# Queueing the last pass's matmuls on TensorE in the order of the source, with the block products begun later and at another pace

## The chip, the cores and the metric

One core of a Trainium2 chip runs the whole kernel. The metric is the time of one execution on the device, in microseconds (us); a kernel is timed in several runs, and the median counts. A profiled execution is one more run, whose trace gives every instruction of the engines: TensorE (PE, with its weight loads as PEld), VectorE (DVE), ScalarE (ACT), GpSimd (POOL) and SyncE (SP), which issues the DMAs.

## What is computed

Three layers follow one another, all in 32-bit floats. The change touches only the last.

1. Retention over 4 x 8 heads of 576 tokens: scores, times a decay that depends on the distance, times v. It gives x, 2304 tokens by 512.
2. A gated layer: `silu(x @ w_gate) * (x @ w_val) @ w_out`, 1536 hidden columns.
3. A squared-ReLU layer on its result:

```python
h = x @ w_in                # 2304 x 512 @ 512 x 2048
r = np.maximum(h, 0.0)
g = r * r
return (g @ w_out)          # 2304 x 2048 @ 2048 x 512
```

## The kernel before, in words

**Arithmetic.** Every 32-bit operand is split into a high part and a low part (`split`: ACT casts the high part, DVE subtracts it for the low part), and a product of two operands is three matmuls: high x high, high x low, low x high. Large products are made by a Strassen-Winograd scheme: seven products of half-size blocks instead of eight, with sums of operands before and sums of results after.

**Passes.** The last layer works through the 2304 tokens in three passes of 768. A pass has eight *systems* (`systems`, one for each 256 hidden columns). The last pass holds the systems 40 to 47, and `turn_over` is 40. A system is seven **slots**, `slot(n, i)` (line 660), i being the number of the Strassen product: six matmuls of 384 columns each, then the evictions. Products 1, 6, 7, 4 build up in a bank called g, 5 and 3 in a bank v, 2 in a bank z; a later product of a bank adds to what is there, so it waits until ACT or DVE has read the bank. Slot 4 and slot 3 complete the two halves of the system's hidden block, tiles caa and cab in the trace (the squared ReLU is a DVE operation).

**The second matrix product of the last pass.** For the other passes it is done by `out2`, in tiles of twelve 512-column matmuls, one or two systems later. For the last pass the systems 40 to 45 are taken in pairs, (40, 41), (42, 43), (44, 45), again by the scheme of seven: a pair is named by its odd system, which this text calls block 41, 43 or 45. Each block has three tiles j of 128 tokens, each with seven **block products**, `out3(n, j, at)` (line 885), of six matmuls of 256 columns: 63 products in all. `PRODUCTS` and `at` give their order. A product's hidden operand is ready when POOL has made four sums of the block's tile (`sums2`, line 865, twelve operations for three tiles), and ACT and DVE have split the tile and the sums (`prepare`, line 874, hs_h and hs_l in the trace). The first product of a tile needs no sum, the second does. There are two buffers for the split tiles, so a tile's splits wait for the last product of the tile two places earlier. The weight operands (wt in the trace) are loaded by DMA (`operands2`, line 826); block 43's go into buffers that block 41's last tile leaves, as its products are done. Each product adds to the bank of the product two places earlier, so it waits until that one's result is evicted (ACT or DVE, xy<-oacc). Systems 46 and 47 are not paired by the scheme: `whole` splits them, and `out4` makes and stores the final output in six pieces, of twelve matmuls of 512 columns (the last piece in halves, twice twelve of 256).

**Order of the work.** The loop of the last pass (line 1103) goes over n = 40 to 48 and writes seven slots in each iteration, partly of system n and partly of n - 1 (three in the last), 59 in all. Iterations 40 and 41 also write nine `out2` tiles of the pass before. After the slot (3, 41), the sixth of iteration 42, the sums and splits of block 41 are written. After each slot, `flow` writes as many block products as a formula allows, which counts slots from `begin_at`:

```python
begin_at = 7 * 3 + START
past = slots["n"] - begin_at
flow(min(int(1.5 * past + 0.7 * max(0, past - 28)), 21 * PAIRED // 2))
```

What is left goes after the loop (`flow(len(stream))`, line 1152).

The written order is not each engine's queue. The framework plans every engine's order itself, on an estimated timeline: where an instruction is not ready in the estimate, a later one that is ready goes first. In the text this is the *planner*. The class `Chained` (line 109) wraps the engines; while `chain["on"]` is set, each instruction is tied behind the one before it on its engine (`issue_after`), so that the written order holds. It is set in the first layer only. `self.last` is the instruction that following ones are tied behind, `self.recent` the latest.

Of the kernel before, what the change touches and what calls it, by code (L numbers as in the profile page):

```python
# [56 lines left out]
PRODUCTS = (1, 5, 6, 3, 7, 2, 4)  # L57
SUMS = (6, 5, 4, 7)
PAIRED = 6
START = 4  # L60


TINY = float(np.uint32(0x38000000).view(np.float32))
# [4 lines left out]
def retention_moe_kernel(  # L68
# [13 lines left out]
    def pool(stack, name, bufs, **kw):  # L82
        return stack.enter_context(
            tc.tile_pool(name=name, bufs=bufs, reuse_waits="tile", **kw)
        )
# [21 lines left out]
    chain = {"on": False}  # L107

    class Chained:


        def __init__(self, engine):
            self.engine, self.last, self.recent = engine, None, None

        def __getattr__(self, name):
            op = getattr(self.engine, name)

            def traced(*args, **kw):
                with ExitStack() as behind:
                    if self.last is not None:  # L120
                        behind.enter_context(tc.issue_after(self.last))
                    i = op(*args, **kw)  # L122
                self.recent = i.ins
                if chain["on"]:
                    self.last = i.ins
                return i

            return traced

    pe, dve, act, pool_e, sp = map(Chained, (nc.tensor, nc.vector, nc.scalar, nc.gpsimd, nc.sync))  # L130
# [219 lines left out]
    def build(n):  # L350

        ph, p, k, what = systems[n]
        if p:
            for x in (0, 3, 2, 1):
                w = operand_tile(n, x)
                sp.dma_start(out=w.bitcast(F32), in_=win[ph, k, what, x])
                yield
                if x != 2:
                    yield
            return  # L360
        w0, w1_ = inputs.pop(n)
        if ph == 1:
            for x in (w0, w1_):
                ensure(x, ready)
            w0, w1_ = ready.pop(w0), ready.pop(w1_)

        def to(x, src):
            if x == 4:
                if ph == 1:
                    built[n, "p"] = w = wb_p.tile([P, 2, 256], F32R, tag="p", name="wb")  # L370
                    split(w[:, 0], w[:, 1], src)
                return
            w = operand_tile(n, x)
            split(w[:, 0], w[:, 1], src)
            later.append((win[ph, k, what, x], w.bitcast(F32)))

        s1 = s1_p.tile([P, 256], F32, tag="s1", name="s1")
        for _ in stationary(w0, w1_, s1, to):
            yield
            while later and n:  # L380
                sp.dma_start(out=later[0][0], in_=later.pop(0)[1])
        if ph == 1:
            loads["held"] -= 2
# [352 lines left out]
    def load_out(n, fs):  # L736
        ph, p = systems[n][:2]
        for f in fs:
            key = (ph, "o", f)
            w = wos[f] = wo_p.tile([P, 2, 512], F32R, tag="wo", name="wo")  # L740
            if p:
                sp.dma_start(out=w.bitcast(F32), in_=wsp[key])
                continue
            if ph == 1:
                ensure(key, ready)
                src = ready.pop(key)
                loads["held"] -= 1
                act.copy(w[:, 0], src)
                pool_e.tensor_tensor(out=w[:, 1], in0=src, in1=f32(w[:, 0]), op=ALU.subtract)
            else:  # L750
                ensure(key, stored)
                sp.dma_start(out=w[:, 1].bitcast(F32), in_=wst[key])
                act.copy(w[:, 0], f32(w[:, 1]))
                tt(out=w[:, 1], in0=f32(w[:, 1]), in1=f32(w[:, 0]), op=ALU.subtract)
            sp.dma_start(out=wsp[key], in_=w.bitcast(F32))
# [70 lines left out]
    def operands2(n):  # L826

        k, x, homes = systems[n][2], n - turn_over, []
        for at, i in enumerate(PRODUCTS):
            if x % 3 == 2:  # L830
                t = t_p.tile([P, 512], F32, tag=f"t{i}", name="wt")
            elif x % 3 and at < 4:
                t = xs_p.tile([P, 512], F32, tag="x", name="wt")
            elif x % 3:
                t = t1_p.tile([P, 512], F32, tag=f"t{i}", name="wt")
            elif at < 4:
                if at % 2:
                    continue
                t = raw_p.tile([P, 1024], U32, tag="raw", name="wt").bitcast(F32)
            else:  # L840
                t = cv_p.tile([P, 512], U32, tag="w", name="wt").bitcast(F32)
            homes.append((t, PRODUCTS[at:at + t.shape[-1] // 512]))
            yield
            for y, i in enumerate(homes[-1][1]):
                w = t[:, 512 * y:512 * y + 512].rearrange("p (y q) -> p y q", y=2)
                moving[n, i] = w.bitcast(F32R)
                src = tsp[k][:, SUMS.index(i)] if i in SUMS else wsp[2, "o", 2 * k + i // 2][:, :, i // 3 * 256:][:, :, :256]
                sp.dma_start(out=w, in_=src)
# [221 lines left out]
    def ready_halves():  # L1070
        while queue and prepared["n"] < flowed["out"] + 2:
            n, j = queue.pop(0)
            (whole if n == end - 1 else prepare)(n, j)
            prepared["n"] += 1

    def follow(n, j, at):
        if at in ("a", "b"):
            out4(n, at, j)
        else:
            out3(n, j, at)  # L1080
            if j == 2:
                for m in (n + 2, n + 3):
                    if m < turn_over + PAIRED:
                        if at == 0:
                            coming[m] = operands2(m)
                            next(coming[m], None)
                        if at % 2 or at > 3 or m % 3 != turn_over % 3:
                            next(coming[m], None)
        if at in (6, "b"):
            flowed["out"] += 1  # L1090
            ready_halves()
# [3 lines left out]
    def flow(upto):  # L1095
        while flowed["n"] < min(upto, len(stream)):
            follow(*stream[flowed["n"]])
            flowed["n"] += 1

    slots["n"] = 0  # L1100
    make2 = iter(())
    begin_at = 7 * 3 + START
    for n in range(turn_over, end + 1):
        tiles = outs.get(n, [])
        seq = [(1, n), (7, n - 1), (2, n), (4, n - 1), (6, n), (3, n - 1), (5, n)]
        if n == turn_over:
            seq = [(7, n - 1), (4, n - 1), (3, n - 1), None, (1, n), (2, n), (5, n), (6, n)]
        make = build(n + 1) if n + 1 < end else iter(())
        for x in fetch.get((n, 0), []):
            load_out(*x)  # L1110
        for x in seq:
            if x is None:
                blocks.close()
                block_pools.append(pool(ctx, "ca_p", 1, side="right"))
                t1_p = pool(ctx, "t1_p", 1, side="right")
                make2 = operands2(n + 1)
                continue
            i, k = x
            if k == end:
                continue  # L1120
            slot(k, i)
            if i == 3 and k >= turn_over and systems[k][2] % 2:
                for j in range(3):
                    if k < turn_over + PAIRED:
                        sums2(k, j)
                    queue.append((k, j))
                ready_halves()
            next(make, None)
            if tiles and (n == turn_over or i in (7, 4, 3)):
                fn, *args = tiles.pop(0)  # L1130
                fn(*args)
            slots["n"] += 1
            next(make2, None)
            past = slots["n"] - begin_at
            flow(min(int(1.5 * past + 0.7 * max(0, past - 28)), 21 * PAIRED // 2))
            if past == 1:
                make2 = operands2(turn_over + 2)
            after(k, i)
            if n == turn_over + 1 and not tiles and t_p is None:
                second.close()  # L1140
                t_p, hl_p = pool(ctx, "t_p", 1), pool(ctx, "hl_p", 2)
                block_pools.append(pool(ctx, "cb_p", 1, side="right"))
        for fn, *args in tiles:
            fn(*args)
        for _ in make:
            pass
        if n == turn_over:
            for _ in make2:
                pass
        if n == end - 1:  # L1150
            load_last(n)
# [62 lines left out]
```

## Time and profile before

| | us |
|---|---|
| median of 3 runs | 877.3 (876.49 to 878.25) |
| profiled execution, its own time | 876.15 |
| its span, first to last instruction | 874.3 |
| PE busy in the span | 862.4 |

The page of the profile gives, for the span of one execution, each engine's busy time and the busy share in 40 slices; the other views group the instructions of a stretch, list them in order of time, say which instruction ended a wait, or follow the chain of waits back from the last instruction. A matmul's start is recorded, its end is modelled, so one matmul's shown time reaches over the start of the next. In a row of a group `x` is the count; then come the busy time, the mean duration in ns, and the idle time of the engine before these instructions with what ended it. In a timeline a row begins with its start and its duration, both in us from the span's start.

### The profile page before, as it was taken

The page shows a single profiled execution, that of the slowest core. Times are in us where ns is not written, and L with a number is a line of the kernel's source. Part 1 is how long each engine was busy: PE and PEld are TensorE (multiplying, and loading weights), DVE is VectorE, ACT ScalarE, POOL GpSimd, SP SyncE. Part 2 cuts the span into 40 slices and gives each one's busy share as a digit, 9 for nine tenths or more (in the row PEclk, how much of TensorE's full clock was granted, in tenths as well). Part 3 has the DMA queues.
Part 4 walks back from the last instruction along what each step waited for, and adds up shares of the span by engine and source line. Part 5 has one row for each costly group of instructions (what it writes and reads, how often), then busy time and mean ns, then how long its engine had stood idle before and what let it go on. Part 6 is the DMA issues. An engine that isn't in the chain of part 4 may idle for free.

```text
span 874.3 us, 14199 instructions
## 1 busy us (share of the span) xinstructions
PE 862.4 (99%) x5226; PEld 751.1 (86%) x5226; DVE 675.5 (77%) x1082; ACT 415.8 (48%) x756; POOL 172.4 (20%) x195
## 2 busy tenths in 40 slices
PE   8999999999999999999999999999999999999998
PEld 7878888888888888888888999889899988999986
DVE  3799999998976998778647999999654566457783
ACT  3677768564553554634335466554244232234321
POOL 3343243123220000000002311132211000062400
PEclk9999999999999999999999999999999999999999
DMA  9994867655653589878744498999989755666432
GB/s 335 402 377 158 280 231 270 243 199 174 217 197 129 175 296 365 304 252 295 249 146 156 165 338 319 357 319 385 386 286 333 250 207 157 222 236 199 164 119 72
DMA packets 87029, 217.81 MB, mean 249 GB/s; under 512 B 8752, under 2 KB 24112, under 8 KB 86960
## 3 DMA queue, kind: packets, MB, share of 16 engines
q1 hardware_dynamic: 86528, 216.50, 70.2%
q8 instruction: 41, 0.67, 0.3%
q10 hardware_dynamic: 432, 0.41, 0.1%
q14 instruction: 28, 0.23, 0.1%
HBM read 146.10 MB, written 70.78 MB: 248 GB/s over the span
## 4 chain that ended last, share of the span: by engine, by line
PE 82%; DVE 7%; DMA 7%; issue 2%; ACT 1%; SPq 0%; DVEq 0%; ACTq 0%
PE oacc L122 40%; PE g L122 24%; PE v L122 12%; PE z L122 6%; DMA k_sb<-in_kv 3%; DVE w L122 3%; DMA wt<-tsp 2%; DMA qk_sb<-in_qk 1%; DVE wi L122 1%; DVE xy L122 1%; DVE xo_l L122 1%; DMA v_sb<-in_kv 1%; DVE hs_l L122 0%; DVE cbg L122 0%; PE o L122 0%
## 5 line engine op out<-in xcount | busy, mean ns | idle before, releaser
L122 PE MATMUL g<-xo_h,wi 128*128 128x384 f32 (+1 forms) x768 | 241.3, 364 | 0.0
L122 PEld LDWEIGHTS g<-xo_h,wi 128*128 128x128 f32 x768 | 142.6, 188 | 16.8
L122 DVE TENSOR_TENSOR xy<-oacc,xy 128x512 f32<-128x512 f32 (+1 forms) x194 | 112.2, 585 | 54.2 <-PE oacc L122 53.5
L122 PE MATMUL oacc<-ho_hi,wo 128*128 128x512 f32 (+1 forms) x480 | 151.1, 370 | 0.5 <-ACT xy L122 0.5
L122 PE MATMUL g<-xo_l,wi 128*128 128x384 f32 (+1 forms) x384 | 139.7, 364 | 0.0
L122 PE MATMUL v<-xo_h,wi 128*128 128x512 f32 (+1 forms) x384 | 124.6, 364 | 0.0
L122 PE MATMUL oacc<-wo,ho_hi 128*128 128x512 f32 x384 | 119.8, 392 | 0.0
L122 PEld LDWEIGHTS oacc<-ho_hi,wo 128*128 128x128 f32 x480 | 88.1, 188 | 17.6 <-ACT xy L122 1.3
L122 PE MATMUL oacc<-ho_lo,wo 128*128 128x512 f32 (+1 forms) x240 | 89.1, 371 | 0.0
L122 PEld LDWEIGHTS oacc<-wo,ho_hi 128*128 128x128 f32 x384 | 71.5, 188 | 12.1
L122 DVE TENSOR_SCALAR w<-w 128x512 f32<-128x512 f32 (+1 forms) x136 | 65.4, 483 | 18.4 <-ACT w L122 17.4
L122 PEld LDWEIGHTS g<-xo_l,wi 128*128 128x128 f32 x384 | 72.1, 188 | 8.6
L122 PEld LDWEIGHTS v<-xo_h,wi 128*128 128x128 f32 x384 | 71.4, 188 | 8.2
L122 PE MATMUL oacc<-wo,ho_lo 128*128 128x512 f32 x192 | 74.3, 393 | 0.0
L122 PE MATMUL v<-xo_l,wi 128*128 128x512 f32 (+1 forms) x192 | 69.9, 364 | 0.0
L122 PE MATMUL z<-xo_h,wi 128*128 128x512 f32 (+1 forms) x192 | 63.0, 365 | 0.0
L122 PEld LDWEIGHTS oacc<-ho_lo,wo 128*128 128x128 f32 x240 | 45.1, 188 | 8.7
L122 ACT ACTIVATE raw<-raw 128x512 uint32<-128x512 uint16 x68 | 46.0, 677 | 13.5 <-DMA raw<-in_w 9.4
L122 DVE SCALAR_TENSOR_TENSOR w<-raw,w 128x512 uint32<-128x512 uint32 x68 | 51.2, 754 | 0.7
L122 DVE CUSTOM_DVE_ANT_0 w<-raw,w 128x1024 uint16<-128x1024 uint16 x68 | 48.7, 716 | 0.8
L122 PE MATMUL oacc<-wt,hs_h 128*128 128x256 f32 x252 | 46.9, 286 | 1.7 <-DVE xy L122 0.6
L122 DVE TENSOR_TENSOR cbg<-v,cbg 128x384 f32<-128x384 f32 (+1 forms) x56 | 34.1, 609 | 18.0 <-PE v L122 10.3
(119 smaller groups left out, 1531.6 us busy)
## 6 DMA issues: line engine op xcount, KB each, us to landing
wi<-win SPq DMA_DIRECT2D x84, 512.0 KB, 5.1
raw<-in_w SPq DMA_DIRECT2D x68, 512.0 KB, 4.8
win<-wi SPq DMA_DIRECT2D x60, 512.0 KB, 3.8
wo<-wsp SPq DMA_DIRECT2D x32, 512.0 KB, 6.0
wsp<-wo SPq DMA_DIRECT2D x28, 512.0 KB, 5.3
qk_sb<-in_qk SPq DMA_DIRECT2D x15, 576.0 KB, 7.2
wst<-w SPq DMA_DIRECT2D x32, 256.0 KB, 6.2
wi<-win SPq DMA_DIRECT2D x28, 256.0 KB, 5.9
```

Source lines behind the costliest of these rows:

```text
L122: i = op(*args, **kw)
```

## The change

`Chained` gets a switch of its own for one engine, and PE's is set at the start of the last pass's loop: from there each matmul is tied behind the one written before it. `START` goes from 4 to 6, so `begin_at` from 25 to 27. The pace of the products was 1.5 a slot, and 2.2 from the 28th slot on; now it is 1.5, then 1.75 after 14 slots and 2.2 after 26. By either formula 55 of the 63 products may be written by the last slot.

```diff
--- before.py
+++ after.py
@@ -57,7 +57,7 @@
 PRODUCTS = (1, 5, 6, 3, 7, 2, 4)
 SUMS = (6, 5, 4, 7)
 PAIRED = 6
-START = 4
+START = 6
 
 
 TINY = float(np.uint32(0x38000000).view(np.float32))
@@ -110,7 +110,7 @@
 
 
         def __init__(self, engine):
-            self.engine, self.last, self.recent = engine, None, None
+            self.engine, self.last, self.recent, self.on = engine, None, None, False
 
         def __getattr__(self, name):
             op = getattr(self.engine, name)
@@ -121,7 +121,7 @@
                         behind.enter_context(tc.issue_after(self.last))
                     i = op(*args, **kw)
                 self.recent = i.ins
-                if chain["on"]:
+                if chain["on"] or self.on:
                     self.last = i.ins
                 return i
 
@@ -1098,6 +1098,7 @@
             flowed["n"] += 1
 
     slots["n"] = 0
+    pe.on, pe.last = True, pe.recent
     make2 = iter(())
     begin_at = 7 * 3 + START
     for n in range(turn_over, end + 1):
@@ -1132,7 +1133,7 @@
             slots["n"] += 1
             next(make2, None)
             past = slots["n"] - begin_at
-            flow(min(int(1.5 * past + 0.7 * max(0, past - 28)), 21 * PAIRED // 2))
+            flow(min(int(1.5 * past + 0.25 * max(0, past - 14) + 0.45 * max(0, past - 26)), 21 * PAIRED // 2))
             if past == 1:
                 make2 = operands2(turn_over + 2)
             after(k, i)
```

## Rows read from the trace of the kernel before

**Rows 1.** The page: busy time by engine, and the granted clock in 40 slices.

```profile
PE 862.4 (99%) x5226; PEld 751.1 (86%) x5226; DVE 675.5 (77%) x1082; ACT 415.8 (48%) x756; POOL 172.4 (20%) x195
...
PEclk9999999999999999999999999999999999999999
```

**Rows 2.** PE's groups from 765.5 us on, by shape (count; busy, mean; idle before).

```profile
L122 PE MATMUL oacc<-wt,hs_h 128*128 128x256 f32 x252 | 46.9, 286 | 1.7 <-DVE xy L122 0.6 <-DMA wt<-tsp 0.5 <-ACT xy L122 0.5
L122 PE MATMUL oacc<-wt,hs_l 128*128 128x256 f32 x126 | 35.1, 284 | 0.2 <-DVE hs_l L122 0.2
L122 PE MATMUL g<-xo_h,wi 128*128 128x384 f32 x85 | 24.3, 335 | 0.0
...
L122 PE MATMUL z<-xo_l,wi 128*128 128x384 f32 x8 | 2.7, 337 | 0.0
```

**Rows 3.** The chain of waits, its last pieces in order of time.

```profile
809.53 7.30 DMA wt<-tsp
...
846.12 1.13 DVE hs_l L122
847.25 0.35 DVE xy L122
...
847.73 8.39 PE oacc L122 x54
...
856.62 14.33 PE oacc L122 x72
```

**Rows 4.** PE's product groups from 833.36 us to the end.

```profile
L122 PE MATMUL oacc<-wt,hs_h 128*128 128x256 f32 x96 | 17.9, 288 | 0.7 <-DVE xy L122 0.6
```

**Rows 5.** PE's timeline: starts of two slots' matmuls, and of seven products'.

```profile
789.77 0.34 PE L122 MATMUL g<-xo_h,wi 128*128 128x384 f32 x1
...
791.86 0.40 PE L122 MATMUL oacc<-wt,hs_h 128*128 128x256 f32 x2
...
810.84 0.64 PE L122 MATMUL oacc<-wt,hs_h 128*128 128x256 f32 x4
...
815.87 0.40 PE L122 MATMUL oacc<-wt,hs_h 128*128 128x256 f32 x2
```

**Rows 6.** Waits of PE from 765.5 us on (us, times, longest).

```profile
PE oacc L122 <- DVE xy L122: 1.2, 3, 0.5
PE oacc L122 <- DMA wt<-tsp: 0.5, 1, 0.5
```

**Rows 7.** Timelines of PE, DVE, POOL and ACT, from 763 to 777 us.

```profile
763.27 0.33 PE L122 MATMUL v<-xo_h,wi 128*128 128x384 f32 x1
...
763.94 0.55 DVE L122 TENSOR_TENSOR cab<-v,cab 128x384 f32<-128x384 f32 x1
...
765.00 0.95 DVE L122 SCALAR_TENSOR_TENSOR cab<-cab 128x768 f32<-128x768 f32 x1
...
766.03 0.75 POOL L122 TENSOR_TENSOR xy<-cab 128x256 f32<-128x256 f32 x1 [99.35 <-DVE cab L122]
...
770.96 2.13 POOL L122 TENSOR_TENSOR xy<-xy,caa 128x256 f32<-128x256 f32 x3
773.06 2.89 POOL L122 TENSOR_TENSOR xy<-caa,xy 128x256 f32<-128x256 f32 x3
...
774.58 2.00 ACT L122 CAST hs_h<-xy 128x1024 fp32r<-128x1024 f32 x2 [0.66 <-POOL xy L122]
...
775.67 2.49 DVE L122 TENSOR_TENSOR hs_l<-xy,hs_h 128x1024 fp32r<-128x1024 f32 x2 [1.72 <-ACT hs_h L122]
...
777.08 0.39 PE L122 MATMUL oacc<-wt,hs_l 128*128 128x256 f32 x1
```

**Rows 8.** DMA issues, 700 to 870 us (count, KB each, us to landing).

```profile
wi<-win SPq DMA_DIRECT2D x23, 512.0 KB, 4.0
wt<-tsp SPq DMA_DIRECT2D x18, 256.0 KB, 5.5
```

**Rows 9.** DVE's timeline: one eviction of a product on time.

```profile
842.47 0.42 DVE L122 TENSOR_TENSOR xy<-oacc,xy 128x256 f32<-128x256 f32 x1 [0.28 <-PE oacc L122]
```

## The prediction

> **What bounds the kernel now.** I read the page first, then PE's groups, PE's timeline, PE's waits, and last the other engines around the first block products. The page says that TensorE (PE) is the bound: it is busy for 862.4 of 874.3 us, at the full clock in every slice [rows 1]. A change of order takes no matmul away, so all that can be won is the time in which PE stands still in the last pass. The page doesn't give that time: the ends of matmuls are modelled, and short waits vanish under them. I work it out from starts.
>
> From 765.5 us, where the first block product starts, PE has 252 + 126 matmuls of products (six each, so 63 products), and in six groups of slots 218 matmuls [rows 2]. The 84 matmuls of the final output are left: 72 of them are one piece of the chain, 14.33 us long, which ends PE's work at 856.62 + 14.33 = 870.95 us [rows 3]. On the way PE doesn't keep the source's order: after its last slot (833.36 us) it still has 96 high-half matmuls, four a product, so 24 products [rows 4]; the source leaves 8 (63 less the 55 that its formula lets go by slot 59). The planner had put slots first wherever a product was not ready in its estimate.
>
> Undisturbed, twelve slot matmuls take 791.86 - 789.77 = 2.09 us, 0.174 each, and seven products 815.87 - 810.84 = 5.03 us, 0.12 a matmul [rows 5]. So a slot is 1.045 us and a product 0.72. Work from 765.5: 378 x 0.12 = 45.3, 218 x 0.174 = 38.0, output 14.3 + 2.9 (the other twelve matmuls at the same rate), together 100.5 us. The stretch is 870.95 - 765.5 = 105.45 us. **PE loses 5.0 us there.** The waits that can be seen say where: products behind the eviction of an earlier one (DVE xy, 1.2 us in three times) and behind a load (0.5 us) [rows 6]. In the part of the last pass before 765.5 us, slots and output tiles of the pass before alone, PE stands in none of these waits.
>
> **The change part by part.** It pins PE in the last pass to the source's order. A matmul whose operand is late now stops everything behind it on PE, slots included. Nothing is added to any engine, and no other queue is pinned, but what DVE, ACT, POOL and SP do when is planned anew around PE's order.
>
> *The waits that can go:* at most the 5.0 us.
>
> *A wait that comes: the first products.* In iterations 40 to 42, seven slots each, the slot (3, 41) is the 20th, and it completes block 41. The new start lets product 0 go behind slot 28 and products 1 and 2 behind slot 29. Product 0 reads only the block itself; product 1 needs the sums that POOL makes of it. Between the end of slot 20 and the first matmul of product 1 that reads a low half PE has nine slots, one product and two matmuls: 9.4 + 0.7 + 0.2 = 10.4 us. The trace of before has that whole way [rows 7]: the slot ends at 763.27 + 0.33 = 763.60; DVE's two operations run at 763.94 and 765.00; POOL starts at 766.03, does nine operations for all three tiles and then the tenth, which the first tile needs; ACT casts at 774.58; DVE subtracts at 775.67; PE has the low half at 777.08. That is 13.5 us, so PE would stand still for 3.1. Before, it did slots meanwhile. The least: DVE's two operations directly behind each other (0.55 + 0.95, 0.6 us saved) and POOL's ten at the 0.71 us of an undisturbed one (2.13 for three; 7.1 instead of 8.55) leave 11.5 us, a wait of 1.1. The most: ACT and DVE each have one more operation of about half a microsecond in front, 4.0. I take 2.9, near the row, because the same operations meet on the same engines; with a depth-first order on POOL it would vanish, but the trace shows breadth-first in this place and the change doesn't touch it.
>
> *Loads.* Weights for (6, 43) go into the buffer that (3, 41) frees, five slots (5.2 us) ahead; they land in 4.0 us [rows 8]. I cost that at nothing: were it late, PE would only spend part of the 2.9 us earlier. The operands of block 43 go into buffers that the last tile of block 41 frees. Between the release by product 15 and the use by product 21 lie five products and four slots, 3.6 + 4.2 = 7.8 us; such a load lands in 5.5 us in the median [rows 8], and took 7.3 where the queue was full [rows 3]. So some are just late: 0.4 us, between 0 and 2. The loads for block 42 are issued two slots later than before and used 13 slots after that: nothing.
>
> *Evictions.* Each product adds onto the bank that the product two places earlier filled, so it waits for that one's eviction. An undisturbed eviction takes 0.42 us and starts right behind its matmuls [rows 9]; back to back products just allow it. With a slot between, as the new order mostly has it, there is 0.72 + 1.05 = 1.77 us for it. That speaks for the change: 55 products get this room, where before 24 had none. Against it: ACT and DVE must also split nine tiles for the products. Where DVE had 1.13 us of subtraction in front of an eviction (0.35), PE's run of products began again only at 847.73 [rows 3], and in the new order such a wait stops slots too; toward the end 2.2 products a slot puts three side by side. Of the 5.0 us of before I give about 2 to the places that go (the run of 24 products) and 0.5 to the loads, and leave **2.5 us**, between 1.0 and 5.0.
>
> *Sum:* 2.9 + 0.4 + 2.5 = 5.8 us of waits in place of 5.0, so +0.8. The profiled execution took 876.15 us (span 874.3 and 1.85 around it); it would take 876.95. The median of the runs is 877.3, 1.15 above the profiled one: **878.1 us**. That is within 0.2% (1.75 us), about what a measurement of this kernel can tell from no change.
>
> *The clock.* PE's longest single wait in the last pass of before was 0.5 us, and the granted clock stayed at its upper level, 2.4 GHz, throughout [rows 1, 6]; the change puts one wait of some 3 us there. The Trainium skill (page "TensorE: Matmul & The Clock Gate", section on the HAM clock gate) says that an idle TensorE is throttled to half its clock until activity releases it. By that rule the sum would be 1 to 8 us more (priced from rows as the third rival below); by the rows it stays as it is, since no wait of such length stands in them. No run so far shows which holds here.
>
> **The rivals.**
> - *Faster.* The sums come early (a wait of 1.1), no load is late, and the slots between the products cover nearly all evictions (1.0): 2.1 us of waits, 2.9 fewer, 874.4 us. For it: PE waits mostly for evictions now [rows 6], and the new order gives room there. Against it: POOL and DVE meet as before. It decides at how early POOL ends.
> - *Slower.* A late eviction stops all of PE: in each of the nine tiles' splits one eviction falls behind a subtraction of some 1.2 us and costs 0.5 (1.13 + 0.35 + 0.3 to start and to resume is just the 1.77 us of room; any operation more is a loss). That is 4.8 us with the end, 3.1 for the first wait, 1.2 for loads: 9.1, 4.1 more than now, 881.4 us. It decides where evictions end later than 1.77 us behind their product. For it: DVE is the second busiest engine and the planner, which hid such waits by taking slots first, no longer may.
> - *The granted clock falls* to 1.2 GHz behind the first wait: each slot would take about another 1.0 us, for one slot up to some eight, as many as lie between two tiles' first products at this pace and a few more: 879 to 886 us. For it: PE has never stood still for so long in this pass. Against it: full clock in all slices [rows 1].
> - *The order doesn't change*, because the planner had chosen the same: rows 4 exclude it but for a detail; 877.3 us.
>
> **How the numbers follow.** The waits change places and the time stays within 0.2%: 0.38 (0.01 of it for an unchanged order). Faster 0.30: the bounds of the first wait and of the evictions reach 3 us down, and rows 6 name just the wait that gets room. Slower 0.32, of it 0.03 for the clock: the first wait is the surest of the terms. The range goes from a little below the faster case to a little above the slower one, 874.0 to 882.2; it leaves out the full 5.0 us gain and the clock's worse half.
>
> **What would show it.** In the changed kernel 8 products, not 24, follow the last slot, which ends some 15 us later. The longest wait of PE in the last pass stands before the second or third block product, ends with DVE's hs_l, and is about 3 us. Waits on wt loads near the first products of block 43 are under 1 us in all. Waits on DVE xy stand near the end. The prediction is wrong if the first wait is missing or longer than 4 us, if waits of PE on evictions sum to over 5 us, or if the granted clock falls below 1.00 behind a wait.

## The result: slower by 8.9 us, and the profile after

The changed kernel took 886.52 us (median of 4 runs, 883.61 to 887.42) against 877.58 for the kernel before (median of 4 runs, one more than in the table of before): a ratio of 1.0097, with an interval from 1.0072 to 1.0123. The profiled execution took 887.42 us, with a span of 885.6, 11.3 more than the 874.3 of before. The page:

```profile
PE 864.7 (98%) x5226; PEld 752.4 (85%) x5226; DVE 676.8 (76%) x1082; ACT 415.6 (47%) x756; POOL 172.4 (19%) x195
...
PEclk9999999999999999999999999999999999999999
```

TensorE (PE) has the same 5226 matmuls and some 2 us more of busy time than in [rows 1]. The clock digits look as full as before, but a digit covers 22 us; below, a finer view shows what they hide.

**The ledger.** The sum of before works for the changed kernel too. The chain of waits (columns: start, duration, what) ends PE's work with its last row:

```profile
765.06 7.20 DMA wi<-win
...
772.30 2.16 PE g L122 x6
...
790.05 0.49 ACT caa L122
...
790.59 1.33 PE g L122 x6
...
805.98 8.36 DMA wt<-tsp
...
814.40 6.17 DMA wt<-tsp
...
852.16 1.47 DVE hs_l L122 x2
...
857.14 0.96 DVE cab L122
...
861.11 21.14 PE oacc L122 x114
```

From 765.5 us to 861.11 + 21.14 = 882.25 are 116.75 us. In them lie 378 matmuls of products at 0.12 us (45.4), 232 of slots at 0.174 (40.4) and the output (17.2): 103.0. PE loses 13.8 us where it lost 5.0. That is +8.8 us in the last pass, as much as the medians differ. The other 2.5 us of the 11.3 come from the first layer, between 57 and 70 us, where the change does nothing (PE waits there on DVE's pl for 2.0 us, before for 0.2); they belong to this one execution.

**Where the 13.8 us are.** PE's waits from 700 us to the end (total, times, longest), to be held against [rows 6]:

```profile
PE g L122 <- ACT caa L122: 3.4, 2, 2.5
PE g L122 <- DMA wi<-win: 2.1, 1, 2.1
PE oacc L122 <- DVE xy L122: 1.8, 4, 0.8
PE oacc L122 <- DVE hs_l L122: 0.8, 1, 0.8
...
PE oacc L122 <- ACT hs_h L122: 0.4, 1, 0.4
...
```

Two of the three longest are new kinds: slots (bank g) that wait for their weights and for a tile caa. PE's timeline has the places (start, duration, instruction, idle before it):

```profile
769.91 0.34 PE L122 MATMUL g<-xo_h,wi 128*128 128x384 f32 x1
772.30 0.56 PE L122 MATMUL g<-xo_h,wi 128*128 128x384 f32 x1 [2.05 <-DMA wi<-win]
...
774.26 0.52 PE L122 MATMUL v<-xo_h,wi 128*128 128x384 f32 x1
774.58 0.52 PE L122 MATMUL v<-xo_l,wi 128*128 128x384 f32 x1
...
776.24 0.33 PE L122 MATMUL v<-xo_l,wi 128*128 128x384 f32 x1
776.41 0.51 PE L122 MATMUL v<-xo_h,wi 128*128 128x384 f32 x2
...
779.39 0.50 PE L122 MATMUL oacc<-wt,hs_h 128*128 128x256 f32 x2 [0.35 <-ACT hs_h L122]
780.65 0.39 PE L122 MATMUL oacc<-wt,hs_l 128*128 128x256 f32 x1 [0.76 <-DVE hs_l L122]
...
787.82 0.28 PE L122 MATMUL oacc<-wt,hs_l 128*128 128x256 f32 x1
790.59 0.44 PE L122 MATMUL g<-xo_h,wi 128*128 128x384 f32 x1 [2.49 <-ACT caa L122]
790.86 0.34 PE L122 MATMUL g<-xo_l,wi 128*128 128x384 f32 x1
...
819.25 0.50 PE L122 MATMUL oacc<-wt,hs_h 128*128 128x256 f32 x2 [0.37 <-DMA wt<-wsp]
...
820.61 0.50 PE L122 MATMUL oacc<-wt,hs_h 128*128 128x256 f32 x2 [0.39 <-DMA wt<-tsp]
...
823.89 0.44 PE L122 MATMUL g<-xo_h,wi 128*128 128x384 f32 x1 [0.89 <-ACT caa L122]
...
854.48 0.50 PE L122 MATMUL oacc<-wt,hs_h 128*128 128x256 f32 x2 [0.79 <-DVE xy L122]
```

And the windows (stretch, its length, then busy time and count of PE, PEld, DVE, ACT and POOL; then the granted clock, the DMA share and GB/s):

```profile
770.00:772.00 2.00, 0.25 (x2) 0.00 (x0) 1.80 (x4) 0.49 (x1) 2.00 (x4) 1.00 1.06 402
772.00:776.00 4.00, 3.70 (x12) 3.70 (x13) 0.00 (x0) 0.48 (x1) 4.00 (x6) 0.57 0.55 219
776.00:778.00 2.00, 2.00 (x16) 2.00 (x15) 1.52 (x2) 0.00 (x0) 0.77 (x2) 1.00 0.30 57
```

In order of time, each counted from start to start against the undisturbed spacing:

1. **The weights of slot (6, 43): 2.2 us.** Their load is issued at 765.06, as slot (3, 41) ends, and lands 7.20 us later; [rows 8] have 4.0 in the median. The DMA engines are full (402 GB/s in 770 to 772). Just ahead on SP's queue, from 755.4 to 763.7, stand the loads of system 42's wt operands, which product 21 is the first to read; product 0 has not begun here. The source writes them only after slot 28; the planner issued them earlier.
2. **The clock: 1.7 us.** Behind that wait the granted clock falls to 1.2 GHz (0.57 of 2.4 GHz in the mean of 772 to 776 us): slot matmuls start 0.32 us apart (774.26, 774.58), from 776.24 on again 0.17. Eleven of them cost 11 x 0.146 = 1.6, those at the edges a little more.
3. **The second product: 1.6 us** (0.35 and 0.76 of it idle).
4. **The slots (6, 44) and (6, 46): 2.65 and 1.15 us**, the two waits on ACT's caa. Slot 6 adds to bank g, which ACT must first have copied into the tile caa of the next block. That tile lies in one of two buffers, and the block two places earlier is still read there: ACT's timeline around it:

```profile
788.01 0.62 ACT L122 CAST hs_h<-caa 128x512 fp32r<-128x512 f32 x1
788.54 0.40 ACT L122 CAST hs_h<-cab 128x256 fp32r<-128x256 f32 x1
788.85 0.36 ACT L122 COPY xy<-oacc 128x256 f32<-128x256 f32 x1
789.11 1.04 ACT L122 CAST hs_h<-xy 128x1024 fp32r<-128x1024 f32 x1
790.05 0.48 ACT L122 COPY caa<-g 128x384 f32<-128x384 f32 x1
```

   The casts split the last tile of block 41. They need a split buffer that the seventh product (product 6) gives up, and START 6 puts product 6 directly ahead of slot (6, 44). So splits, copy and slot follow one another there, and PE stands behind all three. Block 43 repeats it at 823.89.
5. **wt loads of block 43: 1.3 us**, at 819.25 and 820.61, in the chain the loads that take 8.36 and 6.17 us.
6. **Evictions: some 3.7 us**, of it 2.7 between 854 and 864 us. In the two largest of these, at 854.48 and 858.49, the eviction stands behind other work of DVE: subtractions for hs_l (the chain's 1.47 us) and the squared ReLU of cab (0.96).

Together 14.3, half a us above the ledger.

Only the products' tail is as the change writes it. After the last slot, from 856.35 us, the group that answers to [rows 4] is

```profile
L122 PE MATMUL oacc<-wt,hs_h 128*128 128x256 f32 x40 | 7.7, 290 | 0.8 <-DVE xy L122 0.8
```

ten products in place of 24: the two that slot 59 lets go, and the eight left over.

### The profile page after: what moved, and what is told of

Its sections match the earlier page's. It is cut to its first block, busy times and chain, and to the rows that moved or that the text cites. A ratio compares the mean times of both kernels' runs of the same rounds, so it can differ in the third digit from the quotient of the medians.

```text
span 885.6 us, 14194 instructions
## 1 busy us (share of the span) xinstructions
PE 864.7 (98%) x5226; PEld 752.4 (85%) x5226; DVE 676.8 (76%) x1082; ACT 415.6 (47%) x756; POOL 172.4 (19%) x195
## 4 chain that ended last, share of the span: by engine, by line
PE 81%; DVE 8%; DMA 7%; ACT 2%; issue 2%; SPq 0%; POOL 0%; DVEq 0%; ACTq 0%; POOLq 0%
PE oacc L122 39%; PE g L122 23%; PE v L122 12%; PE z L122 6%; DMA k_sb<-in_kv 3%; DVE w L122 3%; DMA wt<-tsp 2%; DVE wi L122 1%; DVE xy L122 1%; DMA wi<-win 1%; PE o L122 1%; DVE hs_l L122 1%; DMA mask_sb<-in_mask 1%; ACT hs_h L122 0%; DMA qk_sb<-in_qk 0%
```

## The experiments

The theory after the first reading was: the pinned order is the cost, since each late operand now stops independent work; the two largest are the tile caa's buffer and the weights of (6, 43) with the clock behind them. The rival was that the later start and the pace cost it. Diffs are against the changed kernel where nothing else is said. The kernel before had medians of 876.81, 877.08 and 877.01 us on the three chips; ratios are to its runs on the same chip.

### The order alone, and the start and pace alone

First the pinned order with the old start and pace, then the kernel before with the new start and pace and no pinning:

```diff
-START = 6
+START = 4
...
-            flow(min(int(1.5 * past + 0.25 * max(0, past - 14) + 0.45 * max(0, past - 26)), 21 * PAIRED // 2))
+            flow(min(int(1.5 * past + 0.7 * max(0, past - 28)), 21 * PAIRED // 2))
```

> The order alone: PE pinned as in the change, START 4 and the old pace. Theory (the order costs, through four places where PE now stands still): the wait for the weights of (6, 43), 2.2 us, and the 1.6 us of half clock behind it stay; product 6 comes two slots earlier, so the wait of (6, 44) for ScalarE's copy (2.65 us) goes and that of (6, 46) shrinks; the wait before the second product grows by about 2 us. About 885 us, clearly slower than before (877.6). Rival A (the later start and the new pace cost, the order is harmless): 877 to 879.

> Start and pace alone: START 6 and the new pace, PE not pinned. Theory: the planner fills every wait with other matmuls as before, 876 to 879 us, waits of PE in the last pass of 5 to 6 us in all. Rival A (start and pace are the cost): 884 to 887.

The order alone: 884.8 us, ratio 1.0087 [1.0069, 1.0104]. Start and pace alone: 878.85, 1.0020 [1.0007, 1.0032]. The order is the cost: 8.0 us by the medians, against at most 2.8 for start and pace, by the upper end of the interval. With START 4 product 6 is done two slots earlier, and there is no wait on ACT's caa; but the second product comes two slots earlier too, so it waits longer for its sums, as PE's waits show:

```profile
PE g L122 <- DMA wi<-win: 2.6, 1, 2.6
...
PE oacc L122 <- DVE hs_l L122: 1.8, 1, 1.8
```

### A third buffer for the tile caa

```diff
-            home = block_pools[k // 2 % 2]
...
-                home.tile([P, 2, 2, M[2]], F32, tag=f"g{x}", name=f"ca{x}") for x in "ab"
+                block_pools[at[k // 2]].tile([P, 2, 2, M[2]], F32, tag=f"g{x}", name=f"ca{x}")
+                for x, at in (("a", (0, 1, 2, 0)), ("b", (0, 1, 0, 1)))
...
+                block_pools.append(pool(ctx, "cc_p", 1, side="right"))
```

> The changed kernel with a third buffer for one of the two tiles of a hidden block (caa), so that the copy of slot (1, 44) does not wait until block 41's last tile is split, nor (1, 46) for block 43's. Theory: the waits of (6, 44) and (6, 46), 2.65 and 1.15 us, go: 886.5 - 3.8 = 882.7 us. Rival B (PE's waits only move on, because ScalarE and VectorE are late everywhere): the same sum of waits at other places, 885.5 us or more.

882.63 us, 1.0063 [1.0044, 1.0081]. PE's waits on ACT's caa went from 3.4 us to none, and the time is lower by 3.9 us by the medians, 3.0 by the ratios. By the ledger the last pass loses 11.0 us instead of 13.8 (PE's work ends at 878.04, with 224 matmuls of slots from 765.5 us on): item 4 is gone, but the wait before (6, 43) is longer in this execution, 3.36 us idle instead of 2.05. So item 4, put at 3.8, is the buffer.

The same edit in the kernel before, as a control:

> The kernel before with the third block buffer. Theory: the planner has gone round that buffer's wait already, so nothing changes: 876 to 878.5 us. If the buffer had cost the planned order something too: up to 1.5 us less.

877.65, 1.0007 [0.9993, 1.0022]: no difference. While the planner orders PE, the buffer costs nothing; the pinned order made it a wait.

### The weights of (6, 43)

First their own buffer (without the third one), so that the load needn't wait for slot (3, 41):

```diff
-        w = wi_p.tile([P, 2, 256 * len(ROWS[x])], F32R, tag=f"wi{x}", name="wi")
+        home = block_pools[2] if (n, x) == (43, 1) else wi_p
+        w = home.tile([P, 2, 256 * len(ROWS[x])], F32R, tag=f"wi{x}", name="wi")
...
+                block_pools.append(pool(ctx, "wx_p", 1, side="right"))
```

> The changed kernel with a buffer of its own for the weights of slots (6, 43) and (3, 43), so that their load does not wait for slot (3, 41). Theory: PE does not stand still before (6, 43), 2.2 us less, and the granted clock stays 1.00 in the stretch that had 0.57, 1.6 us less; of these 3.8 us up to 2 come back before the second product, to which PE now comes earlier: 883 to 884.5 us. Rival B: nothing is won, 885.5 us or more. Rival C (the fall of the clock has another cause than this wait): the half clock stays, and 1.6 us with it.

886.37 us, 1.0112 [1.0091, 1.0133]: a miss, nothing won. The wait for the weights is gone, but PE only reaches the next one earlier. PE's timeline:

```profile
775.14 0.51 PE L122 MATMUL oacc<-wt,hs_h 128*128 128x256 f32 x2 [2.15 <-ACT hs_h L122]
...
776.51 0.39 PE L122 MATMUL oacc<-wt,hs_l 128*128 128x256 f32 x1 [0.86 <-DVE hs_l L122]
...
787.96 0.69 PE L122 MATMUL g<-xo_h,wi 128*128 128x384 f32 x1 [2.49 <-ACT caa L122]
```

The second product now stands still for 3.0 us, and the clock falls twice, behind this wait and at that of (6, 44), as the windows show:

```profile
778.00:782.00 4.00, 4.00 (x20) 4.00 (x19) 0.97 (x2) 0.85 (x2) 0.00 (x0) 0.65 0.00 0
...
787.00:790.00 3.00, 2.04 (x6) 2.04 (x7) 2.31 (x4) 0.91 (x2) 0.00 (x0) 0.61 0.28 112
```

So this run alone doesn't rule out rival C.

Then, on top of the third buffer, the other way: PE is given twelve matmuls ahead of that slot whose result nothing reads, 2.1 us of work (12 x 0.174).

```diff
+            if (i, k) == (6, turn_over + 3):
+                o = out_bank()[:, :M[2]]
+                for _ in range(12):
+                    pe.matmul(o, built[k, 1][:, 0, :P], xo[1][0][:, 0], start=True, stop=True)
```

> The kernel with the third block buffer (882.6 us), and in it twelve matmuls of 384 columns, whose result nobody reads, in PE's queue just before slot (6, 43): 2.1 us of work in the 2 to 3.5 us in which PE stands still there. Theory (the half clock is a consequence of standing still): the granted clock stays 1.00 behind (6, 43), about 1.6 us less, 881 us. Rival C (the clock falls for another reason, such as the weights' load): the half clock stays, 882.6 us or a little more.

879.81 us, 1.0021 [1.0006, 1.0036]: with more work, some 3 us less than the kernel with the third buffer alone. PE's timeline and window there:

```profile
767.69 2.24 PE L122 MATMUL oacc<-xo_h,wi 128*128 128x384 f32 x12
...
770.53 0.44 PE L122 MATMUL g<-xo_h,wi 128*128 128x384 f32 x1 [0.60 <-DMA wi<-win]
```

```profile
772.00:774.00 2.00, 2.00 (x15) 2.00 (x13) 1.05 (x2) 1.30 (x2) 2.00 (x4) 1.00 0.71 193
```

In this execution the clock stays up throughout the last pass, though the load is still late: that speaks for standing still as the cause of the half clock. The runs agree: eight of the ten have a mean clock of 0.999 or 1.000, where the four with the third buffer alone have 0.997 or 0.998. The idle wait of 3.4 us is replaced by 2.1 of work and 0.6 of idle time, which wins 0.7 at most; the larger part is the clock (some 1.7 us). The rest is in smaller waits, at the second product (1.1 us before the edit, 0.4 with it) and on wt loads (0.6 and none); for those I have no separate run.

### The loads in another order, and a later start

Third buffer again; SP's loads for system 42 are tied behind the weights of (6, 43):

```diff
                 sp.dma_start(out=w.bitcast(F32), in_=win[ph, k, what, x])
+                wi_load[n, x] = sp.recent
...
-                sp.dma_start(out=w, in_=src)
+                with ExitStack() as behind:
+                    if x == 2:
+                        behind.enter_context(tc.issue_after(wi_load[n + 1, 1]))
+                    sp.dma_start(out=w, in_=src)
```

> The changed kernel with the third block buffer and with block 42's operand loads tied behind the weights of (6, 43); start and pace as in the change. Theory: the weights land in time and PE does not stand before (6, 43); it comes to the second product earlier and stands there for about 3.3 us, as in the run with a weight buffer of its own, and the half clock may follow there (1.6 us): 880.5 to 882.5 us against 882.6 with the third buffer alone. Rival C (the wait before (6, 43) has nothing to do with those loads): that wait of 2 to 3.5 us stays, 882.6 us.

880.82 us, 1.0040 [1.0030, 1.0051]. The wait for the weights is gone, so the planner's early wt loads had made it; against the third buffer alone that is worth 1.8 us by the medians, 2.0 by the ratios. What the prediction called the first wait now stands alone in PE's timeline:

```profile
776.12 0.50 PE L122 MATMUL oacc<-wt,hs_h 128*128 128x256 f32 x2 [2.12 <-ACT hs_h L122]
...
777.48 0.39 PE L122 MATMUL oacc<-wt,hs_l 128*128 128x256 f32 x1 [0.87 <-DVE hs_l L122]
```

3.0 us together, and in this execution the clock did not fall behind it:

```profile
776.00:778.00 2.00, 1.02 (x6) 0.81 (x7) 1.90 (x2) 1.01 (x2) 0.35 (x1) 1.00 1.00 399
```

Its mean clock over the span is 0.998 all the same: the one fall of this execution lies in the first layer (0.97 in the mean of 50 to 100 us). All ten runs have 0.996 or 0.998; where the clock fell in the other nine, no trace shows.

That wait should shrink if the products begin two slots later. On top of the late loads:

```diff
-START = 6
+START = 8
...
+            flow(min(int(1.85 * past), 21 * PAIRED // 2))
```

> As the run before, and START 8 with 1.85 products a slot (product 0 behind slot 30, product 1 behind slot 31; 55 products by slot 59). Theory: two slots more lie in front of the second product, so the wait there is about 1 us, nothing is left that lets the clock fall, and what stays is evictions (4 us) and up to 1 us of loads: 877 to 879 us, within 0.3% of before. Rival B (waits only move on): 881 us or more.

879.25 us, 1.0020 [1.0008, 1.0032], a little above what was expected. The first wait is down to 0.8, the clock is full; what is left are mostly evictions and one load (PE's waits):

```profile
PE oacc L122 <- DVE xy L122: 1.7, 3, 0.9
PE oacc L122 <- ACT xy L122: 1.2, 1, 1.2
PE oacc L122 <- DMA wt<-tsp: 0.9, 1, 0.9
PE oacc L122 <- DVE hs_l L122: 0.8, 1, 0.8
...
```

But the waits have only moved on, as rival B said, though the time is not rival B's. With the late loads alone ACT xy was 0.2 and wt 0.3, and by the ledger the last pass loses as much in both profiled executions: 7.2 us with the late loads (PE's work ends at 874.42, 225 matmuls of slots), 7.1 here (873.29, 219). Where the 1.6 us between the two medians come from is not shown; the profiled execution before this one had its fall of the clock in the first layer, this one has none.

### Three more with START 9

Third buffer, START 9 and a pace of 1.9 (`int(1.9 * past)`); then the late loads added; then, without the late loads, the pinning only from slot 29 on (`pe.on, pe.last = True, pe.recent` moved ahead of that slot). In these three the third tile of block 41 is computed with block 43's sums, whose region is rewritten before that tile's splits are written; the amount of work is the same, but the splits wait for those later sums (in the first of the three POOL ends them at 799.0 us, and ACT casts them from 799.83 on), which is where their waits of 1.3 us on ACT's hs_h and about 1.0 on DVE's hs_l come from.

> The kernel with the third block buffer (882.6 us), START 9 and a pace of 1.9 a slot, so that the first product goes behind slot 31 instead of 28, with 55 products again by slot 59. Theory: the wait before the second product, 1.6 us here, goes; the wait before (6, 43) and the half clock behind it stay; evictions at the end cost as much as before or up to 1 us more: 881 to 882 us. Rival B (waits only move on): 882.6 us or more.

> As the run with START 9, and the seven loads of block 42's operands are tied on SP's queue behind the weights of (6, 43), before which the planner had issued them in a full DMA queue. Theory: all three early waits and the half clock go; what is left is late loads of block 43 (about 1 us) and evictions (about 4 us), as much as before loses: 876.5 to 879 us, no longer to be told from before. Rival B: 881 us or more, the waits come back elsewhere.

> As the run with START 9, but PE is pinned only from slot 29 on; up to there the planner orders freely. Theory: the planner goes round the wait before (6, 43), so there is no half clock either: 876.5 to 879 us. Rival B: 881 us or more.

They took 885.72 (1.0088 [1.0061, 1.0114]), 882.4 (1.0059 [1.0042, 1.0076]) and 881.85 us (1.0063 [1.0040, 1.0087]), all above what was expected and in the range of rival B. The waits just named are a part of it. What they tell apart is the difference among them. The first has the weights' wait and the half clock behind it (its windows):

```profile
774.00:776.00 2.00, 2.00 (x10) 2.00 (x9) 0.00 (x0) 0.48 (x1) 2.00 (x4) 0.62 0.39 156
776.00:778.00 2.00, 2.00 (x8) 2.00 (x7) 1.13 (x2) 0.00 (x0) 0.62 (x1) 0.53 0.26 18
```

The other two have no half clock in the last pass and at most 0.3 us of the weights' wait, and took 3.3 and 3.9 us less. The weights' wait needs both, PE pinned there and the wt loads ahead: taking either away is enough.

No kernel of the study beats the kernel before. Taken together, the time comes down step by step: 1.0097 as changed, 1.0063 with the third buffer, 1.0040 with the late loads, 1.0020 with START 8. The first two steps each take away a wait that the trace names; of the last that isn't shown.

## Why the prediction was wrong

Forecast were 878.1 us and, as likeliest, no difference; measured were 886.52, above the range. What failed is the sum of PE's waits: 5.8 us forecast, 13.8 found by the ledger. The largest miss is a wait that the sum didn't have, on the buffer of the tile caa; the next is the clock, put at nothing. By its steps:

**Right.** What bounds the kernel, and the 5.0 us that PE lost before: the same ledger gives 13.8 after, and the difference of 8.8 is about that of the medians. That no more than these 5.0 could be won was not put to the test; no run was faster than before. The order did change, with eight products left over for the end; the last slot came 23.0 us later (at 833.36 before, 856.35 after) where some 15 were forecast. About 10 of them are the fourteen products that now lie ahead of it, the other 13 delay: 2.5 from the first layer, the rest waits of the last pass. The start and pace alone moved little.

**"The first products", 2.9 us: right in size, hidden at first.** In the changed kernel the second product stands still for 1.6 us only, since PE had lost time before it. With the weights on time the wait is 3.0 us (late loads), and with a later start 0.8.

**"Loads": the sentence held, the price didn't.** It said that a late load for (6, 43) would only spend part of the first wait earlier. Its own buffer for the weights showed that: the wait moved to the second product, the clock fell all the same, and nothing was won. But I took the landing from the median row, 4.0 us in [rows 8], though SP's timeline of before has the seven loads for system 42 from 753.8 to 761.5 us, ahead of it on the queue; it took 7.2. The prediction counted these seven loads from the slot where the source writes them and put them at nothing; tying them behind the weights took the wait away. And two waits of 2.2 and 1.6 make 3.8 where 2.9 were allowed. Block 43's loads, 0.4 forecast, were 1.3, within their bounds of 0 to 2.

**"The clock", put at nothing and given 0.03 of a chance: this step failed.** The clock fell behind a wait of 2.1 us in the changed kernel, at a price of 1.7 us, within what the third rival named. It was one of the signs by which the prediction said it would be wrong. Another sign, that the longest wait ends with DVE's hs_l, failed too: the longest, 2.49 us, ends with ACT's caa. The Trainium skill (page "TensorE: Matmul & The Clock Gate", section "The HAM clock gate") has an idle TensorE throttled to half its clock; that rule was set aside because no row of before had such a wait, which is no evidence against it. The runs bear it out in part: the granted clock was 0.57 in 772 to 776 us, behind an idle wait of 2.05 us, but 1.00 behind the one of 2.49 before slot (6, 44).

**Not listed at all: 3.8 us, the largest miss.** The prediction names the buffers of the weights, and the description of the kernel those of the split tiles, but neither has the two buffers of the tile caa. They became the largest term, because START 6 puts product 6 ahead of slot (6, 44). The third buffer took it away.

**"Evictions", 2.5 us between 1.0 and 5.0: too low, within its bounds.** They cost about 3.7. They do not sit where the slower rival put them, at every tile: 2.7 us are at the end, between 854 and 864 us, where products stand two and three side by side. There the kind of wait is that rival's, an eviction behind other work of DVE. The prediction's forecast that waits on DVE's xy lie near the end held. I did not try to remove them alone.

The sum by the same terms, measured against forecast: 2.2 + 1.6 for weights and first products (2.9), 1.7 for the clock (nothing), 3.8 for the tile's buffer (nothing), 1.3 for loads (0.4), 3.7 for evictions (2.5): 14.3 where 5.8 were forecast. The slower rival (881.4) had the right side, with another mechanism.

## What to carry to other kernels

Pinning an engine's order turns each late operand into a stop for all that is independent of it, so the question before pinning is not which waits it takes away but which buffers anything in the new order can be late for: the operand tiles, the loads with what is queued ahead of them, and the tiles into which evictions write. What the planner still orders on the other queues (here SP's early loads) is planned for its own estimate; it must be tied too, or PE left free there. And a wait of a few us on PE is priced at the wait plus what a lower clock may take behind it (1.7 us here).

## What the runs showed of the hardware

The fall of the granted clock does not follow a wait's length alone. In the last pass it came behind waits of 2.05 us (the changed kernel), 3.36 (the third buffer) and 3.33 (START 9). Where the weights had their own buffer it came behind the pair of 2.15 and 0.86, and again at the wait of 2.49. With the order alone it came not behind the wait of 2.64 us at 771.30 but at the later one of 1.75 (at 777.20; granted 0.70 in 776 to 778). It did not come behind the same wait of 2.49 us before slot (6, 44) in the changed kernel (790.59 and 790.86 above are 0.27 apart, 0.174 from there on), nor behind 2.12 and 0.87 in the kernel with late loads, nearly the pair just named. Of the changed kernel's four runs one had a mean clock of 1.000, and it is the fastest: 883.61 us, against 886.21 to 887.42 at 0.996 to 0.998. But such a mean does not say where the clock fell: with the late loads the profiled execution had its fall in the first layer, and single runs of the kernel before also have 0.997 or 0.998. Why some waits are followed by it and others not stays open.

A load of 512 KB, landing in 4.0 us in the median, took 7.2 where the DMA engines moved some 400 GB/s.
